# A rewritten head of a fused attention and two-layer kernel: parameters with the first keys, another order of loads and of TensorE's work, and the low parts of weights on GpSimd

## Chip, cores and metric

One core of one Trainium2 chip runs the whole program. The metric is device microseconds (us) of one execution; a profiled execution gives, beside its time, a span from its first to its last instruction and a trace of every engine. Engines are named as in the rows: PE is TensorE (PEld its weight loads), DVE is VectorE, ACT is ScalarE, POOL is GpSimd, SP is SyncE, which issues most transfers.

## The reference

Sliding-window attention with a few sink keys, then two dense blocks. Everything is in float32; the weights come in float64 and the two parameters as 64-bit integers (4 and 128 here).

```
B, H, S, D = 2, 8, 768, 64
scores = q @ k.T / sqrt(D)
keep = (key < n_sink) | ((query - key >= 0) & (query - key < window))
a = softmax(where(keep, scores, -1e9))           # with 1e-9 added to the sum
x = (a @ v), heads side by side                  # 1536 tokens x 512
h = x @ w_in                                     # 512 -> 2048
x = (relu(h) ** 2) @ w_out                       # 2048 -> 512
h = x @ w_in2
out = (P(h) / (Q(|h|) + 1e-6)) @ w_out2          # P cubic, Q quadratic
```

## The kernel before

**Tiling.** Tokens are cut into six segments of 256 (two blocks of 128 query rows), taken in three groups of 512 tokens. Attention works in units: one segment and one pair of heads (128 rows of x, chunk c of four). Group 0 has eight units; with two segments to a group, units 0 and 1 make chunk c = 0, units 2 and 3 chunk 1, and so on. Even units here begin a sequence (their first block sees 128 keys, the second 224), odd units see 224 keys in both blocks. Groups 1 and 2 are done later, in small steps among the dense matmuls of the group before.

**Precision.** A float32 product is made of three matmuls of high and low parts (gemm1_part, L476 to L478: whi by xhi, whi by xlo, wlo by xhi). So every x and every weight block is split. A weight block of 128x512 is converted from float64 in four steps (w_steps): top (ScalarE, L130), wt (VectorE, a shift and an or, L135), whi (ScalarE, L448), wlo = wt - whi (VectorE, L451). For x: high (ScalarE, L249) and low (VectorE, L253).

**The head** (L676 to L722) is the part that does the eight units of group 0, before the dense part starts. On ScalarE, VectorE and TensorE its instructions run in the order in which the program writes them (manual_schedule); GpSimd and SyncE are ordered by the framework's scheduler, and so is the dense part on ScalarE and VectorE. In step k of the loop, in this order: high of x of unit k-2; four masked maxima of unit k (VectorE, L203), which need the unit's scores; two exponentials (ScalarE, L209); one zero fill (L400) and the transposes of unit k-1 on TensorE (L226), copied out by ScalarE and VectorE (L231); two more exponentials; low of unit k-2; those parts of the first dense product (f = 0 and 1, chunk c) whose chunk satisfies c < (k-1) // 2 and whose weights are converted; the values of unit k-1 (L245); the scores of unit k+1 (L189); one step of a weight conversion (go); the sums of unit k and its scaling, first blocks on GpSimd and second blocks on VectorE (L220); two more steps of the conversion; from k = 1 to 7 the first step of the next conversion (begin). So seven conversions run in the head. When one ends, the next weight block is loaded.

**Before the loop.** SyncE issues keys and values of units 0 to 3 in turn, and then three weight blocks of 512 KB. The two parameters (nsw) come in a small transfer of their own on ScalarE's queue, spread to all partitions. setup builds the masks m0, m1, m2 from positions and parameters, mostly on VectorE (L300 to L331). TensorE runs 16 matmuls on zeros (fill, L400) and then the scores of unit 0.

**After the loop.** high and low of the last unit, and the parts that are left (both f, chunk 3), and then the dense part: for each f one first product (its first matmul at f = 2 here), ReLU and square (act1), and the second product two steps of f later. There the remaining weight blocks are converted, two for each f, while ScalarE and VectorE also serve the units of group 1. For such a conversion w_split may hold its instructions back behind an attention step recorded in va_hist.

## Time and profile before

| what | us |
|---|---|
| median of 3 runs (lowest, highest) | 628.69 (627.56, 628.84) |
| the profiled execution, its own time | 627.8 |
| its span, first to last instruction | 625.9 |
| busy: PE, DVE, ACT, POOL | 608.2, 412.8, 407.7, 112.9 |
| mean granted TensorE clock | 0.996 |

The span is what the rows below divide; 1.9 us of the execution's own time lie outside it. Ends of matmuls are modelled, so the busy time of PE is an upper figure. The shares of the whole span say little about the head, which is about a thirteenth of it.

### The profile page before, as it was taken

The page shows a single profiled execution, that of the slowest core. Times are in us where ns is not written, and L with a number is a line of the kernel's source. Part 1 is how long each engine was busy: PE and PEld are TensorE (multiplying, and loading weights), DVE is VectorE, ACT ScalarE, POOL GpSimd, SP SyncE. Part 2 cuts the span into 40 slices and gives each one's busy share as a digit, 9 for nine tenths or more (in the row PEclk, how much of TensorE's full clock was granted, in tenths as well). Part 3 has the DMA queues.
Part 4 walks back from the last instruction along what each step waited for, and adds up shares of the span by engine and source line. Part 5 has one row for each costly group of instructions (what it writes and reads, how often), then busy time and mean ns, then how long its engine had stood idle before and what let it go on. Part 6 is the DMA issues. An engine that isn't in the chain of part 4 may idle for free.

```text
span 625.9 us, 9412 instructions
## 1 busy us (share of the span) xinstructions
PE 608.2 (97%) x3465; PEld 485.6 (78%) x3465; DVE 412.8 (66%) x832; ACT 407.7 (65%) x838; POOL 112.9 (18%) x119
## 2 busy tenths in 40 slices
PE   7878999999999999999999999999999999999996
PEld 3556777777777777888888888888888888888884
DVE  5987787564333333247666469988998887877773
ACT  4778888575644444377777557777686666766662
POOL 2220101010000100030000013334234332222221
PEclk9999999999999999999999999999999999999999
DMA  8946576562222110023655300000010000100002
GB/s 292 302 147 205 181 271 208 190 198 59 79 59 71 52 30 30 2 67 135 203 201 183 121 1 0 2 0 1 2 67 1 1 1 0 69 0 1 0 2 71
DMA packets 19347, 54.80 MB, mean 88 GB/s; under 512 B 2528, under 2 KB 3808, under 8 KB 19296
## 3 DMA queue, kind: packets, MB, share of 16 engines
q1 hardware_dynamic: 19008, 54.01, 26.0%
q8 instruction: 29, 0.48, 0.3%
q14 instruction: 22, 0.18, 0.1%
q10 hardware_dynamic: 288, 0.13, 0.1%
HBM read 50.99 MB, written 3.15 MB: 86 GB/s over the span
## 4 chain that ended last, share of the span: by engine, by line
PE 89%; DVE 5%; ACT 3%; issue 1%; DMA 1%; DVEq 0%
PE b L476 14%; PE b L477 14%; PE b L478 13%; PE b L534 7%; PE b L536 7%; PE b L535 7%; PE b L497 7%; PE b L502 6%; PE b L498 6%; PE b L245 3%; PE b L189 2%; PE b L226 2%; DVE p L203 1%; ACT p L209 1%; DVE wt L135 1%
## 5 line engine op out<-in xcount | busy, mean ns | idle before, releaser
L476 PE MATMUL b<-xhi,whi 128*128 128x512 f32 x256 | 102.7, 402 | 1.4 <-ACT xhi L249 1.4
L477 PE MATMUL b<-xlo,whi 128*128 128x512 f32 x256 | 100.3, 392 | 3.6 <-DVE xlo L253 3.6
L478 PE MATMUL b<-xhi,wlo 128*128 128x512 f32 x256 | 99.9, 390 | 0.0
L525 POOL TENSOR_TENSOR glo<-t,ghi 128x512 fp32r<-128x512 f32 x34 | 48.4, 1424 | 228.9 <-ACT ghi L524 117.1
L488 DVE TENSOR_TENSOR glo<-b,ghi 128x512 fp32r<-128x512 f32 x48 | 33.2, 691 | 69.0 <-ACT b L487 68.8
L497 PE MATMUL b<-ghi,whi 128*128 128x512 f32 x192 | 76.7, 400 | 0.0
L498 PE MATMUL b<-ghi,wlo 128*128 128x512 f32 x192 | 74.9, 390 | 0.0
L535 PE MATMUL b<-wlo,ghi 128*128 128x512 f32 x192 | 74.7, 389 | 0.0
L534 PE MATMUL b<-whi,ghi 128*128 128x512 f32 x192 | 74.5, 389 | 0.0
L536 PE MATMUL b<-whi,glo 128*128 128x512 f32 x192 | 68.5, 389 | 0.0
L209 ACT ACTIVATE p<-p,mn 128x224 f32<-128x224 f32 (+1 forms) x96 | 44.0, 461 | 35.0 <-DVE mn L203 34.9
L220 POOL TENSOR_SCALAR p<-p,sums 128x224 f32<-128x224 f32 (+1 forms) x48 | 27.4, 582 | 217.6 <-DVE sums L215 158.9
L451 DVE TENSOR_TENSOR wlo<-wt,whi 128x512 fp32r<-128x512 f32 x64 | 44.0, 688 | 26.7 <-ACT whi L448 26.4
L477 PEld LDWEIGHTS b<-xlo,whi 128*128 128x128 f32 x256 | 48.1, 188 | 13.9 <-DVE xlo L253 4.9
L476 PEld LDWEIGHTS b<-xhi,whi 128*128 128x128 f32 x256 | 48.1, 188 | 12.6 <-ACT xhi L249 1.5
L448 ACT CAST whi<-wt 128x512 fp32r<-128x512 f32 x64 | 39.6, 619 | 26.2 <-PE b L477 15.3
L478 PEld LDWEIGHTS b<-xhi,wlo 128*128 128x128 f32 x256 | 48.0, 188 | 10.2
L130 ACT CAST top<-st 128x512 f16<-128x512 bf16 x64 | 49.6, 774 | 4.8 <-DVE wt L135 3.1
L502 PE MATMUL b<-glo,whi 128*128 128x512 f32 x192 | 52.2, 392 | 0.0
L478 PE MATMUL b<-yhi,wlo 128*128 128x512 f32 x128 | 49.8, 389 | 0.0
L476 PE MATMUL b<-yhi,whi 128*128 128x512 f32 x128 | 49.8, 389 | 0.0
L477 PE MATMUL b<-ylo,whi 128*128 128x512 f32 x128 | 49.8, 389 | 0.0
(128 smaller groups left out, 1181.7 us busy)
## 6 DMA issues: line engine op xcount, KB each, us to landing
st<-w SPq DMA_DIRECT2D x64, 512.0 KB, 3.4
vv<-att SPq DMA_DIRECT2D x12, 448.0 KB, 3.4
raw<-att SPq DMA_DIRECT2D x12, 352.0 KB, 3.1
out<-o SPq DMA_DIRECT2D x8, 256.0 KB, 2.0
raw<-att SPq DMA_DIRECT2D x6, 272.0 KB, 3.9
vv<-att SPq DMA_DIRECT2D x6, 256.0 KB, 4.1
raw_e<-att SPq DMA_DIRECT2D x4, 352.0 KB, 5.3
vb<-att SPq DMA_DIRECT2D x4, 256.0 KB, 4.7
```

The source lines that it names most:

```text
L130: nc.scalar.copy(top.bitcast(F16).rearrange("p (n w) -> p n w", w=2)[:, :, 1], head)
L209: self.f.lastA = self.nc.scalar.activation(p, p, AF.Exp, scale=-1.0, bias=self.mn[i, k], accum_out=self.sums[:, j : j + 1])
L476: nc.tensor.matmul(h[:, :n], whi[:, cs], xhi[:, c, :n], start=(c == 0), stop=False)
L477: nc.tensor.matmul(h[:, :n], whi[:, cs], xlo[:, c, :n], start=False, stop=False)
L478: nc.tensor.matmul(h[:, :n], wlo[:, cs], xhi[:, c, :n], start=False, stop=(c == NC - 1))
L497: nc.tensor.matmul(acc[m], whi[:, ms], ghi, start=(f == 0), stop=False)
L498: nc.tensor.matmul(acc[m], wlo[:, ms], ghi, start=False, stop=False)
L502: nc.tensor.matmul(acc[m], whi[:, ms], glo, start=False, stop=(f == NF - 1))
L525: self.lastL = nc.gpsimd.tensor_tensor(glo, t3, ghi.bitcast(F32), op=ALU.subtract)
L534: nc.tensor.matmul(acc[t], ghi[:, ts_], whi, start=(f == 0), stop=False)
L535: nc.tensor.matmul(acc[t], ghi[:, ts_], wlo, start=False, stop=False)
L536: self.lastM = nc.tensor.matmul(acc[t], glo[:, ts_], whi, start=False, stop=(f == NF - 1))
```

## The change

- The parameters are appended to the first unit's keys (four words on each partition) and arrive with them; their own transfer is gone.
- The loads before the loop go in the order of FIRST: k is the next unit's keys and queries, v the next unit's values, w a weight block. The three weight loads in step 0 are gone from there.
- The masks: positions outside the causal range are set to a large distance ahead of the parameters (far), so that one comparison with the window does both tests. first_mask (two parameter steps, a copy, m0) stands after the scores of unit 0; second_mask after the second maximum of unit 0, with m1 on VectorE and m2 on GpSimd.
- The zero fills: 6 instead of 16 ahead of the first scores, 8 instead of 1 ahead of the transposes of unit 0, and 3 new ones ahead of its values.
- The parts of the first product follow c < (k-2) // 2, a unit later; in the last step high, low and the rest of the parts stand directly behind the values of the last unit. That pair of instructions is recorded in va_hist.
- Conversions begin in steps 0 to 6 instead of 1 to 7, and in the head their last step (wlo) is done by GpSimd. In the dense part it stays on VectorE.
- Small tiles: nsw and neg are gone, pad (32 bytes on each partition) and up are new, nabs is made earlier.

Left out of the diff: the other path of the program for other parameters, which reads the same packed array, and bookkeeping of widths and arguments.

```diff
@@ -44,6 +44,7 @@
 PER = 3
 HEAD = 2
 DEPTH = 4
+FIRST = "kkvkwvkwvwv"
 NALT = 4
 LAG = 2
 LAG2 = 3
...
@@ -109,7 +116,10 @@
             s = r.start
             vv += [np.concatenate([pad, x[:NSK], x[s : s + D]], axis=0) for x in heads]
             vv += [np.concatenate([x[s - D : s], x[:NSK], pad], axis=0) for x in heads]
-        parts += [np.concatenate(kq, axis=0).reshape(-1), np.concatenate(vv, axis=1).reshape(-1)]
+        kq = np.concatenate(kq, axis=0)
+        if not parts:
+            kq = np.concatenate([kq, np.tile(nsw.view(kq.dtype), (P, 1))], axis=1)
+        parts += [kq.reshape(-1), np.concatenate(vv, axis=1).reshape(-1)]
     return np.ascontiguousarray(np.concatenate(parts))
 
...
@@ -280,12 +290,11 @@
         for top in self.tops:
             nc.gpsimd.memset(top, 0)
         self.ident = c.tile([P, P], F32, name="ident")
-        self.nsw = c.tile([P, 4], I32, name="nsw")
         self.nswf = c.tile([P, 4], F32, name="nswf")
+        c.tile([P, 8], F32, name="pad")
         self.par = c.tile([P, 2], F32, name="par")
         self.ab = c.tile([P, 6], F32, name="ab")
-        io = self.io
-        nc.scalar.dma_start(self.nsw, io["nsw"].bitcast(I32).partition_broadcast(P))
+        self.nabs = c.tile([P, 2], F32, name="nabs")
         make_identity(nc, self.ident)
...
                        allow_small_or_imprecise_dtypes=True)
         v = nc.vector
-        f = self.nswf
-        t = c.tile([P, 2], F32, name="neg")
-        v.tensor_copy(f, self.nsw)
-        lo = f.rearrange("p (s w) -> p s w", w=2)[:, :, 0:1]
-        hi = f.rearrange("p (s w) -> p s w", w=2)[:, :, 1:2]
-        t3 = t.rearrange("p (s w) -> p s w", w=1)
-        p3 = self.par.rearrange("p (s w) -> p s w", w=1)
-        v.tensor_scalar(t3, lo, 0.0, 4294967296.0, op0=ALU.is_lt, op1=ALU.mult)
-        v.tensor_tensor(t3, t3, lo, op=ALU.add)
-        v.scalar_tensor_tensor(p3, in0=hi, scalar=4294967296.0, in1=t3, op0=ALU.mult, op1=ALU.add)
-        ns, win = self.par[:, 0:1], self.par[:, 1:2]
+        lo_, hi_ = slice(0, D), slice(D, P)
+        sk, skh = slice(P, KB), slice(D, D + NSK)
+        for rows, cs, x in ((lo_, slice(KB, WQ), NSK), (hi_, slice(0, D), -D), (hi_, slice(D + NSK, WQ), NSK - D)):
+            v.tensor_scalar_add(rel[rows, cs], rel[rows, cs], float(x))
+        for t in (rel0, rel):
+            far = tmp("wlo4_1", t.shape[-1])
+            v.tensor_scalar(far, t, 0.0, BIG, op0=ALU.is_lt, op1=ALU.mult)
+            v.tensor_tensor(t, t, far, op=ALU.max)
+        v.memset(rel[lo_, sk], BIG)
         self.m0 = c.tile([P, P], F32, name="m0")
         self.m1 = c.tile([P, WQ], F32, name="m1")
         self.m2 = c.tile([P, WQ], F32, name="m2")
-        self.nabs = c.tile([P, 2], F32, name="nabs")
-        m0, m1, m2 = self.m0, self.m1, self.m2
-        out, fut0, fut = tmp("wlo4_1", P), tmp("whi5_0", P), tmp("wlo5_0", WQ)
-        lo_, hi_ = slice(0, D), slice(D, P)
-        for rows, cs, x in ((lo_, slice(KB, WQ), NSK), (hi_, slice(0, D), -D), (hi_, slice(D + NSK, WQ), NSK - D)):
-            v.tensor_scalar_add(rel[rows, cs], rel[rows, cs], float(x))
-        v.tensor_scalar(fut0, rel0, 0.0, -BIG, op0=ALU.is_lt, op1=ALU.mult)
-        v.tensor_scalar(fut, rel, 0.0, -BIG, op0=ALU.is_lt, op1=ALU.mult)
-        v.tensor_scalar(m0, rel0, win, -BIG, op0=ALU.is_ge, op1=ALU.mult)
-        v.tensor_tensor(m0, m0, fut0, op=ALU.min)
-        v.tensor_scalar(out, col, ns, -BIG, op0=ALU.is_ge, op1=ALU.mult)
-        v.tensor_tensor(m0, m0, out, op=ALU.max)
-        v.tensor_scalar(m2, rel, win, -BIG, op0=ALU.is_ge, op1=ALU.mult)
-        v.tensor_tensor(m2, m2, fut, op=ALU.min)
-        sk = slice(P, KB)
-        v.tensor_copy(m2[hi_, D : D + NSK], out[hi_, :NSK])
-        v.tensor_copy(m1, m2)
-        v.tensor_tensor(m1[lo_, :NSK], m1[lo_, :NSK], out[lo_, :NSK], op=ALU.max)
-        v.memset(m1[lo_, sk], -BIG)
-        v.tensor_copy(m2[lo_, sk], out[lo_, :NSK])
+        raw = self.raw0
+        f, par = self.nswf, self.par
+        lo, hi = (f.rearrange("p (s w) -> p s w", w=2)[:, :, i : i + 1] for i in range(2))
+        t3 = c.tile([P, 2], F32, name="up").rearrange("p (s w) -> p s w", w=1)
+        p3 = par.rearrange("p (s w) -> p s w", w=1)
+        ns, win = par[:, 0:1], par[:, 1:2]
+
+        def first_mask():
+            v.tensor_copy(f, raw[:, raw.shape[-1] - 4 :].bitcast(I32))
+            v.scalar_tensor_tensor(t3, in0=lo, scalar=0.0, in1=hi, op0=ALU.is_lt, op1=ALU.add)
+            v.scalar_tensor_tensor(p3, in0=t3, scalar=4294967296.0, in1=lo, op0=ALU.mult, op1=ALU.add)
+            v.tensor_scalar(rel0, rel0, win, -BIG, op0=ALU.is_ge, op1=ALU.mult)
+            v.scalar_tensor_tensor(self.m0, in0=col, scalar=ns, in1=rel0, op0=ALU.is_ge, op1=ALU.mult)
+
+        def second_mask():
+            m1, m2, G = self.m1, self.m2, nc.gpsimd
+            v.tensor_scalar(m1, rel, win, -BIG, op0=ALU.is_ge, op1=ALU.mult)
+            v.scalar_tensor_tensor(m1[lo_, :NSK], in0=col[lo_, :NSK], scalar=ns[lo_], in1=m1[lo_, :NSK],
+                                   op0=ALU.is_ge, op1=ALU.mult)
+            v.tensor_scalar(m1[hi_, skh], col[hi_, :NSK], ns[hi_], -BIG, op0=ALU.is_ge, op1=ALU.mult)
+            G.tensor_scalar(m2, rel, win, -BIG, op0=ALU.is_ge, op1=ALU.mult)
+            for rows, cs in ((lo_, sk), (hi_, skh)):
+                G.tensor_scalar(m2[rows, cs], col[rows, :NSK], ns[rows], -BIG, op0=ALU.is_ge, op1=ALU.mult)
+
+        self.masks = [first_mask, second_mask]
         nu = 2 * sum(u[2][2] for u in units())
         self.mn = c.tile([P, nu], F32, name="mn")
         self.mn_i = 0
...
         return [f"{p}{c + i}_{k}" for i in range(2) for k in range(2) for p in ("whi", "wlo")]
 
     def att_load(self, u, early, alt):
-        wk, wq = seg_dims(u[2])[:2]
-        w = wk + wq
+        w = raw_width(u)
         if early is not None:
             raw = self.yp.tile([P, self.yw[early]], F32, tag=f"y{early}", name="raw_e")[:, :w]
         else:
             raw = self.att.tile([P, w], F32, tag="raw", name="raw", bufs=2)
         off = self.att_off[u]
+        if not off:
+            self.raw0 = raw
         self.lastD = self.nc.sync.dma_start(raw, self.io["att"][off : off + P * w].rearrange("(p w) -> p w", w=w))
         return raw
 
     def att_load_v(self, u, alt):
         tags = self.alt_tags(alt)
         wk, wq, wa, wb = seg_dims(u[2])
-        off = self.att_off[u] + P * (wk + wq)
+        off = self.att_off[u] + P * raw_width(u)
         src = self.io["att"][off : off + P * (wa + wb)].rearrange("(p w) -> p w", w=wa + wb)
         if alt:
             out = [self.att_tile("va", wa, alt=tags[3]), self.att_tile("vb", wb, alt=tags[4])]
...
@@ -448,7 +461,7 @@
             nc.scalar.copy(out[0], t)
 
         def low():
-            nc.vector.tensor_tensor(out[1], t, out[0].bitcast(F32), op=ALU.subtract)
+            last.tensor_tensor(out[1], t, out[0].bitcast(F32), op=ALU.subtract)
             self.w[(which, f, half)] = tuple(out)
 
         return [lambda: f64_top(nc, st, top), lambda: f64_rest(nc, st, t, top), high, low]
...
         nload = 0
 
-        def prefetch():
+        def prefetch(values=True):
             nonlocal nload
             if nload < len(us):
                 g0 = us[nload][0] == 0
                 early = (None, 0, 1, 2)[nload % DEPTH] if g0 else None
                 u, alt = us[nload], nload % NALT if g0 else 0
-                raws = [self.att_load(u, early, alt), None]
-                if g0:
-                    raws[1] = self.att_load_v(u, alt)
-                loaded.append((u, raws))
+                loaded.append((u, [self.att_load(u, early, alt), None]))
                 nload += 1
+                if g0 and values:
+                    values_of(nload - 1)
+
+        def values_of(i):
+            u, raws = loaded[i - nload]
+            raws[1] = self.att_load_v(u, i % NALT)
 
         n0 = sum(1 for u in us if u[0] == 0)
         done = 0
@@ -645,8 +660,13 @@
             self.w_split(which, f, half)
             wload(which)
 
-        for _ in range(DEPTH):
-            prefetch()
+        for i, what in enumerate(FIRST):
+            if what == "k":
+                prefetch(values=False)
+            elif what == "v":
+                values_of(FIRST[:i].count("v"))
+            else:
+                wload(0)
         self.setup()
 
         self.new_x(0)
@@ -661,9 +681,14 @@
             un[k] = Unit(self, *loaded.pop(0), k % NALT)
             un[k].scores([self.bank(b) for b in SCB[k % 2]])
 
+        def pieces(n):
+            for f, c in [x for x in parts if x[1] < n and (0, x[0], 0) in self.w]:
+                self.gemm1_part(0, f, c, self.x[0], GN[0], hb[f])
+                parts.remove((f, c))
+
         def begin():
             key = cq[0].pop(0)
-            conv.append(self.w_steps(*key))
+            conv.append(self.w_steps(*key, nc.gpsimd))
             conv[0].pop(0)()
 
         def go():
@@ -676,22 +701,23 @@
         pinned = ExitStack()
         pinned.enter_context(tc.manual_schedule(engines={E.PE}))
         with tc.manual_schedule(engines={E.Activation, E.DVE}):
-            self.fill(self.bank(0), 16)
+            self.fill(self.bank(0), 6)
             scores(0)
+            self.masks[0]()
             for k in range(n0 + 1):
                 cur, prev, old = un.get(k), un.get(k - 1), un.get(k - 2)
-                if k == 0:
-                    wload(0, 3)
                 if old:
                     old.high()
                 ex = list(cur.blocks) if cur else []
                 for i, j in ex:
                     cur.maximum(i, j)
+                    if not k and (i, j) == (0, 1):
+                        self.masks[1]()
                 for i, j in ex[:2]:
                     cur.exponential(i, j)
                 if prev:
                     tb = [self.bank(b) for b in (0, 1)]
-                    self.fill(tb[0], 1)
+                    self.fill(tb[0], 8 if k == 1 else 1)
                     for j in range(2):
                         prev.transpose(j, tb[j])
                         prev.copy(j)
@@ -699,13 +725,18 @@
                     cur.exponential(i, j)
                 if old:
                     old.low()
-                for f, c in [x for x in parts if x[1] < (k - 1) // pairs and (0, x[0], 0) in self.w]:
-                    self.gemm1_part(0, f, c, self.x[0], GN[0], hb[f])
-                    parts.remove((f, c))
+                pieces((k - 2) // pairs)
                 if prev:
-                    prev.values(self.bank(SCB[k % 2][0]))
+                    ob = self.bank(SCB[k % 2][0])
+                    if k == 1:
+                        self.fill(ob, 3)
+                    prev.values(ob)
                 if k + 1 < n0:
                     scores(k + 1)
+                if k == n0:
+                    high = prev.high()
+                    self.va_hist.append((prev.low(), high))
+                    pieces(NC)
                 go()
                 if cur:
                     cur.sum()
@@ -713,15 +744,12 @@
                         cur.scale(i, j)
                 go()
                 go()
-                if 0 < k <= NCONV:
+                if k < NCONV:
                     begin()
                 while nload < n0 and len(loaded) < DEPTH - 1 or not loaded:
                     prefetch()
-            un[n0 - 1].high()
-            un[n0 - 1].low()
+            assert not parts
             done = n0
-        for f, c in parts:
-            self.gemm1_part(0, f, c, self.x[0], GN[0], hb[f])
```

## Rows read from the trace of the kernel before

**Rows 1.** Busy time by stretch: engines, granted clock, share of DMA, GB/s.

```profile
8.40:50.60 42.20, 32.26 (x376) 22.33 (x369) 35.33 (x131) 32.13 (x98) 10.05 (x16) 0.96 0.73 249
50.60:90.00 39.40, 38.84 (x246) 30.18 (x246) 29.59 (x72) 34.42 (x78) 3.49 (x6) 1.00 0.68 222
200.00:626.00 426.00, 419.69 (x2025) 344.79 (x2017) 290.55 (x450) 272.39 (x496) 87.24 (x68) 1.00 0.14 47
```

**Rows 2.** Timeline of DVE: start, duration, what, idle before and its releaser.

```profile
5.19 0.17 DVE L300 CAST nswf<-nsw 128x4 f32<-128x4 int32 x1 [2.44 <-DMA nsw<-nsw]
...
6.04 0.29 DVE L320 TENSOR_SCALAR m<-tmp,par 128x128 f32<-128x128 f32 x1
...
8.40 0.28 DVE L203 CUSTOM_DVE_ANT_0 p<-b,m 128x128 f32<-128x128 f32 x1
...
16.32 0.29 DVE L203 CUSTOM_DVE_ANT_0 p<-b,m 128x128 f32<-128x128 f32 x1 [0.71 <-PE b L189]
...
25.02 0.67 DVE L451 TENSOR_TENSOR wlo<-wt,whi 128x512 fp32r<-128x512 f32 x1
...
29.44 0.67 DVE L451 TENSOR_TENSOR wlo<-wt,whi 128x512 fp32r<-128x512 f32 x1
```

**Rows 3.** Loads issued at 0.75 and 3.07: size, us to landing.

```profile
raw<-att SPq DMA_DIRECT2D x1, 272.0 KB, 4.3
...
raw_e<-att SPq DMA_DIRECT2D x1, 272.0 KB, 5.9
```

**Rows 4.** Timeline of PE.

```profile
1.00 6.55 PE L400 MATMUL b<-zero 128*128 128x512 bf16 x16 [1.00 <-POOL zero L277]
...
25.75 1.04 PE L226 MATMUL b<-ident,p 128*128 128x128 f32 x8
...
28.62 0.99 PE L189 MATMUL b<-raw_e 64*64 64x224 f32 x16
...
49.95 0.40 PE L476 MATMUL b<-xhi,whi 128*128 128x512 f32 x1
...
50.65 0.39 PE L476 MATMUL b<-xhi,whi 128*128 128x512 f32 x1
```

**Rows 5.** The chain that ended last: start, duration, what.

```profile
14.79 1.38 PE b L189 x16
...
21.10 0.38 DVE p L203
...
25.73 0.29 DVE p L203
...
30.04 0.38 DVE p L203
...
34.47 0.83 PE b L189 x16
35.37 0.29 DVE p L203
...
39.67 0.38 DVE p L203
```

**Rows 6.** Waits of PE, 0 to 130 us: total, times, longest.

```profile
PE b L477 <- DVE xlo L253: 3.6, 4, 1.1
...
PE b L226 <- DVE mn L203: 0.6, 1, 0.6
```

**Rows 7.** Timeline of POOL in the head.

```profile
11.14 0.78 POOL L220 TENSOR_SCALAR p<-p,sums 128x128 f32<-128x128 f32 x2 [8.57 <-DVE sums L215]
...
20.03 1.30 POOL L220 TENSOR_SCALAR p<-p,sums 128x128 f32<-128x128 f32 x2 [4.10 <-DVE sums L215]
```

**Rows 8.** Busy time in one stretch, columns as in rows 1.

```profile
14.00:17.00 3.00, 3.00 (x34) 2.04 (x31) 1.81 (x9) 1.60 (x6) 0.97 (x2) 0.50 1.04 390
```

**Rows 9.** One line of the kernel on POOL: ns min/median/max, first and last start.

```profile
L525 POOL TENSOR_TENSOR glo<-t,ghi x34: 1287/1302/2165, 356.2 to 611.3; 128x512 fp32r<-128x512 f32 x34
```

**Rows 10.** Timeline of ACT at the head's end.

```profile
47.49 0.76 ACT L130 CAST top<-st 128x512 f16<-128x512 bf16 x1
```

More of the change, by code (lines that the diff above doesn't have):

```diff
@@ L86, in units, with raw_width, pack_attention @@
     return out
-def pack_attention(q, k, v):
+def raw_width(u):
+    wk, wq = seg_dims(u[2])[:2]
+    return wk + wq + (4 if u == units()[0] else 0)
+def pack_attention(q, k, v, nsw):
     qT = q.transpose(0, 1, 3, 2)
@@ L433, in w_split_, with w_steps @@
     def w_split_(self, which, f, half):
-        for step in self.w_steps(which, f, half):
+        for step in self.w_steps(which, f, half, self.nc.vector):
             step()
-    def w_steps(self, which, f, half):
+    def w_steps(self, which, f, half, last):
         nc = self.nc
@@ L567, in run @@
             self.att_off[u] = off
-            wk, wq, wa, wb = seg_dims(u[2])
-            off += P * (wk + wq + wa + wb)
+            off += P * (raw_width(u) + sum(seg_dims(u[2])[2:]))
         self.yw = [NC * GN[0], NC * GN[1], 2 * TG2]
```

18 lines of the change are left out of this document (9 added, 9 removed).

## Prediction

> **What bounds the kernel now.** I read the table of busy time by stretch first [rows 1]. In the last 426 us TensorE is busy for 419.69, so nothing that the change touches in the head can make that part shorter; it can only start earlier. From 50.6 to 90 us TensorE is nearly full too (38.84 of 39.40), with ScalarE at 34.42. In the head, 8.4 to 50.6, TensorE is busy for 32.26 of 42.20 us, VectorE for 35.33: this is where time can be had, and there the order on ScalarE and VectorE is written out by hand, one unit after the other. So I followed one unit's beat, from the first maximum of one unit (L203) to that of the next, and asked of each beat which wait ends last.
>
> The start: VectorE can do nothing with the parameters before 5.19, when their small load has landed, and then runs nineteen small instructions for masks and parameters, so that the first maximum comes at 8.40 [rows 2], although the first scores need only the first key load, landed at 0.75 + 4.3 = 5.05 [rows 3]. TensorE passes that time in 16 zero fills that take 0.41 us each [rows 4]. Matmuls of the same 512 columns advance by 0.23 us later on (three from 49.95 to 50.65) [rows 4], so the fills run at the lower level, 1.2 GHz.
>
> The beats start at 21.10, 25.73, 30.04, 35.37 and 39.67 [rows 5]: 4.63, 4.31, 5.33 and 4.30 us for units 3 to 6. In the odd ones TensorE waits for the low part of x that VectorE has only just made: four such waits, 3.6 us in all [rows 6]. In the even ones VectorE is the limit: it ends its scaling and then subtracts a weight's low part, 0.60 us from its start to that of the next maximum (29.44 to 30.04) [rows 2, 5].
>
> **The change, part by part.** All times are of the profiled execution.
>
> *Start.* The parameters ride with the first keys, so they land at about 5.05 instead of 5.19. Behind them stand three small operations and two of 128 columns instead of nineteen: 5.19 to 6.04 is four such small steps (0.2 each), the wide ones 0.3 each [rows 2], so the first mask is ready at 5.05 + 0.6 + 0.6 = 6.25. The work on positions moves ahead of the landing, into VectorE's idle 2.4 us. Scores of unit 0 start at 5.05; with 6 fills (ended near 3.5) TensorE is then idle for 1.5 us, and I take the lower level, 1.38 us against 0.83 for such 16 matmuls [rows 5]: 6.45, and the first maximum at 6.6, 1.8 us earlier. The second mask puts three operations (about 0.7) between the second and third maximum; the exponentials trail the maxima, so I count 0.4: **-1.4**. Its other half goes to GpSimd, idle there until its scaling. Bounds: three such operations take 1.2 us at 0.39 each (half of the pair of 0.78) [rows 7] and, at 1.3 each, 3.9; even then it is ready at 10.2, when unit 1's maxima need it.
>
> *Loads.* In the new order the first weight block is fifth in the queue, behind 1152 KB. The sixth load now ends the first 1600 KB and lands at 3.07 + 5.9 = 9.0 [rows 3]; the new fifth ends 1664 KB, so 9.2. Now ScalarE takes that block at the end of unit 0, ahead of unit 1's exponentials, at about 9.1 to 9.9. Unit 1's first maximum is due at 10.2. The load is hidden unless it comes later than about 9.9; from there each us costs one, as all exponentials queue behind it.
>
> *Units 1 and 2.* Between 14 and 17 us the granted clock was 0.50 [rows 8], after TensorE had waited for unit 0's scaling, whose GpSimd part starts at 11.14 [rows 7]. The scores in it took 1.38, the same 0.83 later [rows 5]. Eleven new fills (8 ahead of the transposes, 3 ahead of the values) stand in exactly that wait; at 0.41 each the 8 end by 11.5, when the transposes' input is ready from 10.5 and their first copy is due 11.7. I take the full clock from there on: 0.55 from the scores and, by the same ratio, 0.5 from the values, less 0.3 for fills that run over: **-0.7**. The third unit's first maximum then comes at 14.2 instead of 16.32 [rows 2]. Unit 2, 16.32 to 21.10, loses VectorE's 0.60 and the rest of the low clock and is held by TensorE alone, from the transposes to the end of the scores 28.62 + 0.99 - 25.75 = 3.86 [rows 4], about 4.1 with the waits: **-0.7**.
>
> *The low part on GpSimd and the parts of the first product.* VectorE's beat without the subtraction is 25.02 - 21.10 = 3.92 for odd units, 29.44 - 25.73 = 3.71 for even ones [rows 2, 5]. The parts now come one unit later, in even units: the odd ones lose the wait for x, units 3 and 5 go to 3.95: 0.68 + 1.38 = **-2.1**. The even ones now carry six of these matmuls where unit 4 had three. From its transposes at 25.75 to the end of its scores it needed 3.86 us; three more at 0.23 are 0.69, of which 0.1 falls in a wait: 4.45 against 4.31 and 4.30, so **+0.3**. GpSimd takes 1.30 us for such a subtraction (median; longest 2.17) [rows 9]. With its scaling that is 2.1 to 2.8 of 4 us, behind the scaling, and over before the next scaling; nothing waits for the low part in that time.
>
> GpSimd's pair of scalings took 0.78 at 11.14, and 1.30 at 20.03, where VectorE's subtraction with both inputs in SBUF came behind its own scaling [rows 7]. So 0.5 us of the wait ahead of the transposes goes too; that is what keeps the even beat at 4.45. The Trainium skill, SBUF — State Buffer, section "Who interferes with whom", says that a VectorE instruction with two SBUF inputs and a GpSimd instruction that reads SBUF shut each other out for a whole instruction, whoever comes first. By that rule, the trace agrees; it also speaks against this change, since a longer GpSimd instruction now holds what VectorE's scaling and its shift-and-or need. By the rows the sum stays as it is, by the rule at its worst it is the first rival below.
>
> *The end of the head.* Unit 7 loses its parts (beat 3.95). Then transposes 1.04, six matmuls 1.4 in what was a wait for the copies, values 1.15. Before, two ScalarE steps of weights stood ahead of the last xhi (the second 0.76 at 47.49) [rows 10], and TensorE waited; in the new order xhi and xlo follow the values at once, and 2.2 us later the parts are done. From unit 7's first maximum: 3.9 + 3.6 + 2.1 = 9.6 against 50.65 - 39.67 = 11.0 [rows 4, 5]: **-1.4**.
>
> Head: -1.4 - 0.7 - 0.7 - 2.1 + 0.3 - 1.4 = **-6.0**.
>
> *What is late next.* The new last unit does no weight conversion, and none may start ahead of x's last low part. Before, an eighth was under way at 47.49 [rows 10]. The dense part starts one to one and a half conversions poorer. One costs ScalarE 0.76 [rows 10] and about 0.6, so 0 to 2.1 us. TensorE was already a little late there (a wait of 0.6 for a unit's maxima) [rows 6], and ScalarE has 5 us of air in 39.4 [rows 1]. I take **+1.3**. The dropped and added small tiles shift addresses; same-shaped operations show no spread that I could tie to an address, so nothing.
>
> **Sum**: -6.0 + 1.3 = -4.7. The profiled execution took 627.8 (span 625.9 and 1.9 around it) and would take 623.1; the median of the runs is 0.9 above it, 628.69, so **624.0**. A measurement here tells about 0.2% (1.3 us) from no change.
>
> **Rivals.**
> 1. *GpSimd's subtraction shuts VectorE out (slower).* If it is put ahead of the scaling (GpSimd's order isn't written by hand) or runs into the next shift-and-or, VectorE waits up to 1.30 in each of seven units: at 1.0, 7.0 us, so 631. It decides from 4.7 / 7 = 0.67 per unit. Against it: the scaling's input is ready before the weight's high part, and about 1.2 us of air lie between its end and the next shift-and-or.
> 2. *TensorE stays at the lower level.* Ten early fills are gone, and TensorE is idle from 3.5 to 5.05. A unit has some 3 us of TensorE work; at 1.38 / 0.83 that is 2 us more, partly hidden. Up to the end of unit 3: +3.3, so 627.3. For it: one idle stretch was enough for 14 to 17 [rows 8]. Against it: from 5.05 TensorE now has work without a break.
> 3. *The dense part gives it back.* Conversions bind it, and TensorE waits there as long as the head was shortened, but for a us: 628. The wait of 0.6 speaks for it, ScalarE's air against.
> 4. *Nothing is late:* the lag costs nothing and the clock rises at once: 622.
>
> **Chances.** Forecast 0.62 (its own range 622.4 to 626.5: the lag 0 to 2.1, the clock up to unit 2, fills that run over); rival 1 0.08; rival 2 0.12; rival 3 0.12; rival 4 0.06. The range that leaves out rival 1 and the outer parts of 3 and 4: 621.6 to 628.4. Faster by over 0.2% (below 627.4): forecast, rival 4 and four fifths of rival 2, 0.78. Within: 0.14. Slower: 0.08.
>
> **What would show it.** First maximum at 6.6 (not before 8); granted clock of 1 by the first values; beats of 4 us in odd and 4.5 in even units, no TensorE wait for xlo but the last; GpSimd's subtractions at 1.3 right behind its scalings; first matmul of the third gemm block near 44.7 instead of 50.65, and TensorE waits of 1 to 2 us between there and 85. Wrong if VectorE's scaling or shift-and-or stretches above 1 us, if the clock is at 0.5 beyond 12 us, or if those later waits grow to 4.

## The result, and the profile after

| | before | after |
|---|---|---|
| median of 4 runs, us (lowest, highest) | 628.12 (627.36, 628.84) | 622.00 (621.27, 622.59) |
| profiled execution, its span | 627.8, 625.9 | 621.27, 619.4 |
| end of the head's parts, us from the span's start | 50.65 | 44.55 |
| what is left of the span behind that | 575.26 | 574.82 |
| of this: to the start of the last matmul, and behind it | 568.65, 6.6 | 569.01, 5.8 |

The ratio is 0.9906 (95%: 0.9888 to 0.9924): faster by 6.1 us of the median, where 4.7 were forecast. The time is in the predicted range (621.6 to 628.4), 2.0 us below the predicted 624.0 and just below the forecast's own range of 622.4 to 626.5. The median before is 628.12 here and was 628.69 when the prediction was made.

In the changed kernel the first maximum is L213, a fill L413, the transposes L236, scores L199, values L255, the parts of the first product L489 to L491, the conversion's four steps L140, L145, L461 and L464, and high and low of x L259 and L263.

Busy time by stretch, the head, what follows it, and the first part of what follows (`44.30:60.00`; columns as in [rows 1]):

```profile
5.33:44.55 39.22, 31.98 (x386) 21.93 (x379) 31.15 (x123) 30.67 (x96) 16.81 (x26) 1.00 0.76 280
44.55:84.00 39.45, 39.31 (x248) 30.55 (x247) 31.38 (x74) 35.63 (x80) 3.71 (x6) 1.00 0.67 225
44.30:60.00 15.70, 15.70 (x82) 12.47 (x81) 12.23 (x28) 15.46 (x33) 1.17 (x2) 1.00 0.60 204
```

The like stretch of the kernel before, as long and as far from the end of its head:

```profile
50.40:66.10 15.70, 15.70 (x82) 12.45 (x80) 11.04 (x25) 12.78 (x29) 1.32 (x2) 1.00 0.58 189
```

Against [rows 1] the head (from the first maximum on) is 3 us shorter, GpSimd does 6.8 us more in it and VectorE 4.2 less. Behind it TensorE is as full as it was (39.31 of 39.45). From the end of the head to the last matmul the kernel now takes 0.36 us more, with one new wait for ScalarE (four of 16 scores start at 84.75, the other twelve at 85.39). At the very end it takes 0.8 us less, because the last store lands sooner (before, then after):

```profile
85.39 0.81 PE L199 MATMUL b<-raw 64*64 64x128 f32 x12 [0.20 <-ACT x L408]
```

```profile
out<-ot SPq DMA_DIRECT2D x1, 128.0 KB, 3.7
```

```profile
out<-ot SPq DMA_DIRECT2D x1, 128.0 KB, 2.8
```

The change doesn't touch that store, and it took between 2.8 and 3.7 us in the fourteen traces of this document. So the span, 6.5 us shorter, gained 6.1 in the head, lost 0.4 behind it and owes 0.8 to the last store.

The start, on VectorE and TensorE, and two loads in the chain of waits, the first keys and the fourth weight block (the last two lines: start, duration, what):

```profile
3.52 0.17 DVE L327 CAST nswf<-raw 128x4 f32<-128x4 int32 x1 [0.48 <-DMA raw<-att]
...
5.33 0.29 DVE L213 CUSTOM_DVE_ANT_0 p<-b,m 128x128 f32<-128x128 f32 x1 [0.15 <-PE b L199]
```

```profile
1.00 2.74 PE L413 MATMUL b<-zero 128*128 128x512 bf16 x6 [1.00 <-POOL zero L287]
3.67 1.45 PE L199 MATMUL b<-raw 64*64 64x128 f32 x16
...
6.02 1.90 PE L413 MATMUL b<-zero 128*128 128x512 bf16 x8
9.23 0.91 PE L236 MATMUL b<-ident,p 128*128 128x128 f32 x6 [1.31 <-POOL p L230]
```

```profile
0.75 2.75 DMA raw<-att
...
13.92 7.79 DMA st<-w
```

The first keys are there at 3.50, not at 5.05 as in [rows 3]. From there to the first maximum it takes 1.83 us (3.39 before), and scores, not masks, end last, by little: the mask is ready at 5.17. The pace of the scores is still that of the lower level, 1.45 for 16 against 0.83 (the column of the granted clock reads 1.00 from the start, so here the pace has to tell).

GpSimd and VectorE around the first maxima of unit 3, and the waits of TensorE from 0 to 130 us:

```profile
16.40 0.78 POOL L230 TENSOR_SCALAR p<-p,sums 128x128 f32<-128x128 f32 x2 [1.63 <-DVE sums L225]
17.15 1.27 POOL L464 TENSOR_TENSOR wlo<-wt,whi 128x512 fp32r<-128x512 f32 x1
```

```profile
19.27 0.68 DVE L145 SCALAR_TENSOR_TENSOR wt<-st,top 128x512 int32<-128x512 int32 x1
```

```profile
PE b L255 <- ACT pT L241: 4.2, 5, 1.1
PE b L236 <- POOL p L230: 2.1, 2, 1.3
...
PE b L489 <- ACT xhi L259: 0.5, 1, 0.5
PE b L199 <- ACT x L408: 0.2, 1, 0.2
```

The subtraction follows the scaling at once, takes 1.27 and ends at 18.42, 0.85 us before VectorE's shift-and-or, which keeps its 0.68. The pair of scalings takes 0.78, as at 11.14 in [rows 7]. The four waits for xlo of [rows 6] are gone; the one for xhi is the only such wait left.

The head by the prediction's steps (first maximum of each unit; a unit's beat runs from its first maximum to that of the next):

| step | before | after | predicted change | measured |
|---|---|---|---|---|
| first maximum of unit 0 | 8.40 | 5.33 | -1.8 | -3.07 |
| first maximum of unit 2 | 16.32 | 13.14 | -2.1 | -3.18 |
| beat of unit 2 | 4.78 | 4.07 | -0.7 | -0.7 |
| beat of unit 3 | 4.63 | 3.93 | -0.7 | -0.7 |
| beat of unit 4 | 4.31 | 5.15 | +0.1 | +0.8 |
| beat of unit 5 | 5.33 | 3.93 | -1.4 | -1.4 |
| beat of unit 6 | 4.30 | 4.62 | +0.2 | +0.3 |
| unit 7's first maximum to the end of the parts | 10.98 | 9.69 | -1.4 | -1.3 |
| end of the head to the last matmul | 568.65 | 569.01 | +1.3 | +0.4 |
| last matmul to the end of the span | 6.6 | 5.8 | 0 | -0.8 |

Four rows are off: the start, unit 4 and the last two. One experiment or more stands against each of the first three. In the start, unit 0's beat grew by 0.68 (3.21 to 3.89), where the prediction counted 0.4 for the second mask. Unit 4's is in the timeline of ScalarE:

```profile
21.79 0.79 ACT L140 CAST top<-st 128x512 f16<-128x512 bf16 x1 [1.19 <-DMA st<-w]
...
22.70 0.40 ACT L219 ACTIVATE p<-p,mn 128x128 f32<-128x128 f32 x1
```

The first maximum was there at 21.15, but its exponential is queued behind the first step of the fourth weight block, issued at 13.92 and landed 7.79 us later, at 21.71.

### The profile page after: what moved, and what is told of

It reads as the page before. It is cut to its first block, busy times and chain, and to the rows that moved or that the text cites. A ratio compares the mean times of both kernels' runs of the same rounds, so it can differ in the third digit from the quotient of the medians.

```text
span 619.4 us, 9428 instructions
## 1 busy us (share of the span) xinstructions
PE 605.4 (98%) x3465; PEld 484.4 (78%) x3465; DVE 408.3 (66%) x821; ACT 406.8 (66%) x838; POOL 120.7 (19%) x129
## 4 chain that ended last, share of the span: by engine, by line
PE 87%; ACT 6%; DVE 3%; DMA 2%; issue 1%; POOL 0%; DVEq 0%; ACTq 0%
PE b L489 14%; PE b L490 13%; PE b L491 13%; PE b L548 7%; PE b L547 7%; PE b L549 7%; PE b L510 7%; PE b L515 6%; PE b L511 6%; PE b L255 3%; PE b L236 2%; PE b L199 2%; ACT p L219 2%; ACT top L140 1%; DMA st<-w 1%
## 5 line engine op out<-in xcount | busy, mean ns | idle before, releaser
L489 PE MATMUL b<-xhi,whi 128*128 128x512 f32 x256 | 102.7, 402 | 0.5 <-ACT xhi L259 0.5
L491 PE MATMUL b<-xhi,wlo 128*128 128x512 f32 x256 | 99.9, 390 | 0.0
L230 POOL TENSOR_SCALAR p<-p,sums 128x224 f32<-128x224 f32 (+1 forms) x48 | 24.4, 519 | 202.1 <-DVE sums L225 130.4
L489 PEld LDWEIGHTS b<-xhi,whi 128*128 128x128 f32 x256 | 48.1, 188 | 11.8 <-issue 1.3
L464 DVE TENSOR_TENSOR wlo<-wt,whi 128x512 fp32r<-128x512 f32 x57 | 39.3, 689 | 25.9 <-ACT whi L461 25.5
L491 PEld LDWEIGHTS b<-xhi,wlo 128*128 128x128 f32 x256 | 48.1, 188 | 10.4
L461 ACT CAST whi<-wt 128x512 fp32r<-128x512 f32 x64 | 39.6, 619 | 22.5 <-PE b L490 15.3
L140 ACT CAST top<-st 128x512 f16<-128x512 bf16 x64 | 49.6, 775 | 5.8 <-DVE wt L145 4.6
L491 PE MATMUL b<-yhi,wlo 128*128 128x512 f32 x128 | 49.8, 389 | 0.0
L489 PE MATMUL b<-yhi,whi 128*128 128x512 f32 x128 | 49.8, 389 | 0.0
```

The lines of the kernel that those rows point to most:

```text
L140: nc.scalar.copy(top.bitcast(F16).rearrange("p (n w) -> p n w", w=2)[:, :, 1], head)
L489: nc.tensor.matmul(h[:, :n], whi[:, cs], xhi[:, c, :n], start=(c == 0), stop=False)
L491: nc.tensor.matmul(h[:, :n], wlo[:, cs], xhi[:, c, :n], start=False, stop=(c == NC - 1))
```

## The experiments

Theory: the head sets all. The parameters with the keys, the low part on GpSimd, the parts a unit later and the fills each shorten it, and ScalarE's air makes up the late conversions. Rivals: the gain is one part's alone; GpSimd's work shuts VectorE out; the clock falls; the dense part gives back; addresses count. Spans and head ends are of one profiled execution of each kernel; ratios are to the kernel before, run on the same chip. A ratio is uncertain by about 0.18%, so two kernels that lie within some 1.6 us of each other are told apart by their traces alone. Three parts of the change were not undone alone: the order of the loads, the shorter masks and the new order in the last step of the head. What they brought is read from the changed kernel's trace and not shown by a run.

**The low part back on VectorE.**

```diff
-            conv.append(self.w_steps(*key, nc.gpsimd))
+            conv.append(self.w_steps(*key, nc.vector))
```

> Only the subtraction of the weights' low parts goes back to VectorE in the head; all else stays as changed. If VectorE's length is what the change relieved: the beats of units 2 to 6 grow by 0.4 to 0.6 us each, GpSimd's pair of scalings takes 1.3 again instead of 0.8, and the whole is 2 to 3 us slower than the changed kernel (span 621.5 to 622.5). Rival, ScalarE's order sets the beat and VectorE was only next to it: beats within 0.1, whole within 0.5 us (span 619 to 620).

624.23 us, ratio 0.9937 (0.9921 to 0.9953). The beats of units 1 to 6 are 4.51, 4.28, 4.52, 4.56, 4.53, 4.55. In four of them the next maximum follows VectorE's subtraction at once; those of units 4 and 6 end with scores or GpSimd's scaling, 0.1 to 0.2 us behind it. Odd units lose 0.6 us; of the even ones only unit 2 loses (0.2), so the expected 0.4 to 0.6 for each did not come. GpSimd's scalings are slow again, as the pair of 1.30 in [rows 7], and TensorE waits six times for them where it waited twice:

```profile
26.39 0.67 DVE L464 TENSOR_TENSOR wlo<-wt,whi 128x512 fp32r<-128x512 f32 x1
```

```profile
25.92 1.30 POOL L230 TENSOR_SCALAR p<-p,sums 128x128 f32<-128x128 f32 x2 [3.03 <-ACT whi L461]
30.53 1.46 POOL L230 TENSOR_SCALAR p<-p,sums 128x224 f32<-128x224 f32 x2 [3.31 <-ACT whi L461]
```

The head ends at 47.77, 3.2 later: 1.36 up to unit 7's first maximum and 1.86 behind it. Some of the latter is not the edit: there the granted clock was 0.73 (39 to 42.5 us) and 0.70 (to 45), and six parts took 2.5 us instead of 1.6. The ratios give 1.9 us for the edit, as much as for the sixteen fills below and more than for the other three parts of the head that were undone alone (0.6 to 1.3).

**The parts of the first product a unit earlier, as before.**

```diff
-                pieces((k - 2) // pairs)
+                pieces((k - 1) // pairs)
```

> Only the rule for the parts of the first product goes back to c < (k-1) // 2. If the wait for the low part of x was worth what the prediction says: TensorE waits about 1 us for xlo again in units 3, 5 and 7, the even units lose 0.3 to 0.5, whole +1.5 to +2.5 us (span 621 to 622). Rival, the matmuls are only moved from one beat to the next: within 0.5 us of 619.4.

622.89 us, 0.9918 (0.9901 to 0.9935); head 46.55, 2.0 later. Beats of units 3 and 5 are 5.35 and 5.36, 1.4 longer each, those of units 4 and 6 are 0.3 and 0.6 shorter, and the waits for x are back:

```profile
PE b L490 <- DVE xlo L263: 3.4, 3, 1.1
```

So the step "parts a unit later" holds in kind, and in the traces in size; the ratios differ by 0.8 us only, which they can't tell from 2.

**Fewer fills: one ahead of the first transposes, none ahead of the values.**

```diff
-                    self.fill(tb[0], 8 if k == 1 else 1)
+                    self.fill(tb[0], 1)
-                        self.fill(ob, 3)
+                        self.fill(ob, 0)
```

> Only the fills of the second step go back (1 and 0 instead of 8 and 3); the first 6 stay. If they hold the clock: granted clock 0.5 for 3 to 4 us somewhere between 9 and 16 us, scores of unit 2 at 1.4 instead of 0.83, first maximum of unit 2 about 1 us later, whole +1 us (span 620.4). Rival, the clock holds without them: no stretch at 0.5, and the whole is 0 to 0.5 us faster, as transposes and values need not queue behind them.

622.79 us, 0.9916 (0.9899 to 0.9933). The profiled execution is the longest of its six; its head ends at 47.66, with beats of 4.95 and 6.70 in units 1 and 2:

```profile
11.00:13.00 2.00, 1.93 (x24) 1.65 (x28) 1.52 (x5) 2.00 (x7) 0.46 (x1) 0.50 1.05 401
13.00:15.00 2.00, 2.00 (x21) 1.16 (x14) 1.05 (x8) 0.89 (x5) 1.74 (x3) 0.50 1.07 388
15.00:18.00 3.00, 2.62 (x23) 2.10 (x23) 1.98 (x6) 1.94 (x8) 0.00 (x0) 0.50 0.75 273
```

The clock is at 1.2 GHz from about 10.5 us, after TensorE had been 2.05 us without work, to beyond 20. The ratios make it 0.6 us, and the other five executions are 0.5 to 2.1 us shorter than the profiled one, so not every execution need pay the whole price.

**The small spread load back.** Four words to each partition, on ScalarE's queue as in the kernel before, into a new tile that nothing reads.

```diff
+        spare = c.tile([P, 4], I32, name="spare")
+        nc.scalar.dma_start(spare, self.io["a"].bitcast(I32).partition_broadcast(P))
         make_identity(nc, self.ident)
```

> A transfer of 16 bytes, spread to all partitions, is issued on ScalarE's queue at the start as before the change, into a tile that nobody reads; the parameters still come with the keys. If that small transfer was what held the first keys up: they land at about 5 us again instead of 3.5, first maximum at 6.7 instead of 5.33, whole +1 to +1.5 us (span 620.5 to 621). Rival, the new order on SyncE's queue (keys ahead of values) makes the first keys earlier: landing stays at 3.5 and the whole within 0.5 us of 619.4.

625.24 us, 0.9952 (0.9934 to 0.9971): a larger loss than the head shows. The first keys land at 4.90, the head ends 0.9 later (45.45), and what is left behind it is 578.63, 3.8 longer than in the changed kernel (3.0 up to the last matmul, 0.8 behind it, where the last store took 3.4 us). The new tile also moves every tile allocated behind it. So the two were parted.

**The same load, into the 32 bytes of pad, so that no tile moves.**

```diff
-        c.tile([P, 8], F32, name="pad")
+        spare = c.tile([P, 8], I32, name="spare")
+        nc.scalar.dma_start(spare[:, :4], self.io["a"].bitcast(I32).partition_broadcast(P))
```

> The small spread load of the run before it again, but into the 32 bytes of the pad tile, so that no other tile moves. In that run the head ended 0.9 us later and the dense part took 3.8 us more. If the dense part's 3.8 us came from the moved tiles and not from the load: first keys land near 4.9, first maximum near 6.7, head ends at 45.4, the rest takes 574.9 as in the changed kernel, span 620.3. Rival, the load itself disturbs the later part: the rest 578 or more again, span 624.

622.79 us, 0.9926 (0.9908 to 0.9943). The first keys (of these two loads the first; size, us to landing after an issue at about 0.75) need 4.0 us instead of 2.75:

```profile
raw<-att SPq DMA_DIRECT2D x1, 274.0 KB, 4.0
spare<-a ACTq DMA_DIRECT2D x1, 2.0 KB, 4.2
```

The first maximum comes at 6.61 (1.83 behind the landing, as in the changed kernel), the head ends at 45.50, and what is left is 574.95. So the small load alone held the keys up, for about 1 us of time; the 3.0 us up to the last matmul in the run before came from the moved tiles (1.6 by the ratios), as that stretch is 568.94 here.

**No pad, and a pad that is 512 bytes larger.**

```diff
-        c.tile([P, 8], F32, name="pad")
```
```diff
-        c.tile([P, 8], F32, name="pad")
+        c.tile([P, 8 + 128], F32, name="pad")
```

> Only the pad tile of 32 bytes is taken out; the tiles behind it move down. If TensorE's pace depends on where its operands lie: matmuls of the second block's first product step at 233 ns instead of 227 (384 of them, 2.6 us), and the rest behind the head takes 577 to 579 instead of 574.9 (span 621.5 to 623.5); the head itself unchanged at 44.5. Rival, addresses do nothing and the earlier run's slow part had another cause: 574.9 and a span of 619.4.

> The pad tile is 512 bytes longer, so that everything behind it moves by 512 bytes. If only the place within 512 bytes counts for TensorE's pace: steps at 227 ns, span 619.4 as in the changed kernel. Rival, any move of the tiles away from where they were costs: steps at 233 ns somewhere and a span of 621 or more.

No pad: 625.32 us, 0.9955 (0.9937 to 0.9973), with 578.56 behind the head, 3.7 more, all but 0.1 of it up to the last matmul. Larger pad: 622.07 us, 0.9911 (0.9894 to 0.9927), with 574.87. Groups of TensorE's instructions from 44 us on (busy time and mean ns of one), in the changed kernel, without the pad, and with the larger one:

```profile
L491 PE MATMUL b<-yhi,wlo 128*128 128x512 f32 x128 | 49.8, 389 | 0.0
L489 PE MATMUL b<-yhi,whi 128*128 128x512 f32 x128 | 49.8, 389 | 0.0
```

```profile
L488 PE MATMUL b<-yhi,whi 128*128 128x512 f32 x128 | 50.7, 396 | 0.0
L490 PE MATMUL b<-yhi,wlo 128*128 128x512 f32 x128 | 50.6, 396 | 0.0
```

```profile
L491 PE MATMUL b<-yhi,wlo 128*128 128x512 f32 x128 | 49.8, 389 | 0.0
L489 PE MATMUL b<-yhi,whi 128*128 128x512 f32 x128 | 49.8, 389 | 0.0
```

From start to start these matmuls advance by 226.5 to 227 ns in the changed kernel and with the larger pad, by 233 to 234 without the pad and with the spare tile. There are 384 of them: about 2.5 of the 3.7 us; the rest is spread thinly over others. Moves by 16 and by 32 bytes cost it, a move by 512 bytes doesn't, so what counts repeats after 512 bytes (or 64, 128 or 256, which no run tells apart). Which tile it is wasn't isolated. The kernel before has 389 ns here too: the pad gains nothing, it keeps what the dropped tiles would have lost. (Without the pad the head ended 1.9 later, but 1.6 of that lies behind unit 7's first maximum, where the granted clock was 0.53 from 39 to 42.5 us.)

**The coefficients with the first keys.** Two more small spread loads (a and b of the second block, 2 and 1 KB) are issued at 12.28 and 13.35, ahead of the fourth weight block. Here they ride with the first keys too, six more words on each partition.

```diff
-    return wk + wq + (4 if u == units()[0] else 0)
+    return wk + wq + (10 if u == units()[0] else 0)
...
+            G.tensor_copy(self.ab, raw[:, raw.shape[-1] - 6 :])
             G.tensor_scalar(m2, rel, win, -BIG, op0=ALU.is_ge, op1=ALU.mult)
...
-        nc.sync.dma_start(ab[:, 0:4], io["a"].partition_broadcast(P))
-        nc.sync.dma_start(ab[:, 4:6], io["bb"].partition_broadcast(P))
```

> The six coefficients of the second block also come with the first keys, and GpSimd copies them out; their two small spread loads, issued at 12.3 and 13.4 us in the changed kernel, are gone. If those two hold the queue ahead of the fourth weight block (landed 21.7, for which ScalarE waited 1.2 us and unit 4's beat was 5.15): it lands near 19.7, ScalarE doesn't wait, beat of unit 4 at 4.6, whole -0.5 us (span 618.9). Rival, the queue is full with large loads and the block lands at 21 or later anyway: beat stays at 5.1, span 619.4.

620.96 us, 0.9891 (0.9873 to 0.9909). The weight block is issued at 12.99 and lands at 20.34, 1.4 us earlier, 0.9 of it because it is issued earlier; ScalarE takes it without a wait, unit 4's beat is 4.62 and the head ends at 44.20. The span, 620.0 where 618.9 was expected, doesn't show it: the last store took 3.7 us here and 2.8 in the changed kernel; up to the last matmul (568.92) nothing was lost. The ratios don't tell the two apart. Busy time from 17 to 18 us, the changed kernel first (the last two columns are the share of the DMA engines and GB/s):

```profile
17.00:18.00 1.00, 1.00 (x11) 0.73 (x7) 0.78 (x5) 0.82 (x3) 1.00 (x2) 1.00 0.26 78
```

```profile
17.00:18.00 1.00, 1.00 (x15) 0.74 (x7) 0.72 (x4) 0.81 (x3) 1.00 (x2) 1.00 1.10 416
```

So 3 KB in small pieces left the engines mostly idle for a us in the middle of 512 KB loads. The run with the larger pad, with the program order of the changed kernel, shows the same stall at another length (1.86 and a beat of 5.81).

**The low part subtracted twice on GpSimd**, so that it occupies 2.6 us a unit. It computes the same values.

```diff
+            for _ in range(1 if last is nc.vector else 2):
-            last.tensor_tensor(out[1], t, out[0].bitcast(F32), op=ALU.subtract)
+                last.tensor_tensor(out[1], t, out[0].bitcast(F32), op=ALU.subtract)
```

> GpSimd makes each low part in the head twice, so 2.6 us instead of 1.3 for each unit. If it has air there and does not shut VectorE out: beats within 0.1 of 3.93 and 4.62, head ends within 0.4 of 44.5 us, span 619 to 620. Rival, the two engines hold each other up: the second subtraction lies over VectorE's shift-and-or or over the next scaling, one of these stretches by 0.5 us or more, beats grow by 0.3 to 1.0, head ends at 46.5 to 51.

624.20 us, 0.9950 (0.9934 to 0.9965). GpSimd's two subtractions and VectorE's shift-and-or, in two units:

```profile
18.39 2.62 POOL L465 TENSOR_TENSOR wlo<-wt,whi 128x512 fp32r<-128x512 f32 x2
...
22.95 2.65 POOL L465 TENSOR_TENSOR wlo<-wt,whi 128x512 fp32r<-128x512 f32 x2
```

```profile
20.47 1.09 DVE L145 SCALAR_TENSOR_TENSOR wt<-st,top 128x512 int32<-128x512 int32 x1
...
24.67 1.48 DVE L145 SCALAR_TENSOR_TENSOR wt<-st,top 128x512 int32<-128x512 int32 x1
```

GpSimd is done at 21.01 and 25.60, the shift-and-or 0.55 later in both, nearly its whole 0.68: it did not run slowly, it waited. The Trainium skill, SBUF — State Buffer, section "Who interferes with whom", says that the pair of ports which the two engines share is an exclusive lock, held for the whole instruction by whoever issues first. By that rule the shift-and-or waits until GpSimd is done; the trace agrees, with 0.55 us of it behind that. So rival 1's mechanism exists. It starts when GpSimd's work lasts until the next shift-and-or; the 1.27 of the changed kernel ends 0.85 us ahead of it. The head ends 1.8 later (46.35), of which 1.25 is unit 1's beat of 5.17, at a low clock (below); the beats of units 3 and 5 grew by 0.25 and 0.43, and unit 4's lost its wait for the load (4.62). The ratios make it 2.8: the profiled execution is the shortest of its six, and what the others lost no trace shows.

**An eighth conversion in the head.**

```diff
-NCONV = 7
+NCONV = 8
```

> The last unit's step begins an eighth conversion, so that the dense part starts with one more. If the lag of the conversions costs time in the dense part (the prediction took 1.3 us): the rest behind the head takes 573.5 to 574.3 instead of 574.8, the head at most 0.3 more. Rival, ScalarE makes the lag up by itself: the rest 574.8 as before, whole within 0.4 us of 619.4.

622.11 us, 0.9921 (0.9898 to 0.9943); 574.47 behind the head against 574.82, and 568.79 against 569.01 up to the last matmul. A conversion in stock is worth 0.2 us there, and nothing in the median: a lag of 1.3 isn't there. (The wait for ScalarE at 85 us stays. The head ends 0.6 later, not 0.3 at most, with unit 1's beat at 5.17 at a low clock, below.)

**Sixteen fills ahead of the first scores, as before.**

```diff
-        self.fill(self.bank(0), 6)
+        self.fill(self.bank(0), 16)
```

> Only the first fills go back to 16. If they stand ahead of the first scores as TensorE's order has it: scores of unit 0 at 7.5 instead of 3.67, at the higher level, first maximum at 8.3 to 8.5 instead of 5.33, and with it the head and the whole about 3 us later (span 622.5). Rival, units 1 and 2 win back what the first loses, as the clock is up earlier and the fills of the second step are then too many: +1 us or less.

623.48 us, 0.9938 (0.9915 to 0.9961). The fills end at 6.36, the scores run at the full clock (0.83 instead of 1.45), and the first maximum comes at 7.15 instead of 5.33. That is earlier than the expected 8.3 to 8.5, because the 16 fills took 5.36 us and not the 6.55 of [rows 4]. The head ends 1.3 later: of the 1.8 lost at the start unit 4 gives 0.5 back, as its weight block has landed by then (beat 4.63). The higher level doesn't pay for the wait. (The span is longer by 2.4, as the last store took 3.7 us here too.)

**The best version: coefficients with the keys, and the parts shared out**, those of f = 0 in even and of f = 1 in odd units, where TensorE waits 1.05 us for the copy.

```diff
-        def pieces(n):
-            for f, c in [x for x in parts if x[1] < n and
+        def pieces(n, fs=(0, 1)):
+            for f, c in [x for x in parts if x[0] in fs and x[1] < n and
...
-                pieces((k - 2) // pairs)
+                pieces((k - 2) // pairs, (0, 1) if k == n0 else (k % 2,))
```

> The version with the coefficients in the first keys, and the parts of the first product shared out: f = 0 in even units, f = 1 in the odd unit behind, where TensorE waits 1.05 us for a copy. If the even beats of 4.62 are TensorE's, lengthened by six matmuls, and three of them fit into that wait: beats of units 4 and 6 near 3.95, odd ones unchanged at 3.93, head ends 1.2 to 1.4 us earlier (42.8 to 43.0), whole -1.2 us against that version (span 618 to 618.8). Rival, the three only lengthen the odd beats by as much as they leave the even ones: within 0.3 us of it.

620.64 us, 0.9890 (0.9870 to 0.9910). Even beats are 4.08 (4.62), odd ones stay at 3.94, as expected: 1.1 us. The profiled execution lost 1.2 of it again in unit 1 (5.13, granted clock 0.51 from 11 to 13 us), so its head ends at 44.29. It is the fastest measured, but its interval holds the changed kernel's ratio too.

**The clock in unit 1.** In four traces the beat of unit 1 was 4.95 to 5.17 and the clock 0.50 or 0.51 from 11 to 13 us; in the other nine it was 3.9 to 4.5, at 1.00. The waits of the first transposes part them (the run with two subtractions, then the best version; the changed kernel's, 1.31, is shown with its start):

```profile
3.67 0.88 PE L199 MATMUL b<-raw 64*64 64x128 f32 x16
...
9.24 0.91 PE L236 MATMUL b<-ident,p 128*128 128x128 f32 x6 [2.02 <-POOL p L230]
```

```profile
3.67 1.06 PE L199 MATMUL b<-raw 64*64 64x128 f32 x16
...
9.35 0.91 PE L236 MATMUL b<-ident,p 128*128 128x128 f32 x6 [2.00 <-POOL p L230]
```

In the four (few fills 2.05, eight conversions 1.85, and these two) TensorE was idle for 1.85 to 2.05 us ahead of the transposes, in the other nine for 0.3 to 1.61. In three of the four that came from a good start: the clock rose early, the first scores took 0.83 to 1.06 instead of 1.45, and the eight fills, a fixed number, were through sooner. No run changed the idle time alone, and at the head's end the clock fell in two traces after waits (1.05 and 0.84) that the changed kernel has at the same place without it. So what decides is left open.

## Why the prediction was right, and where its sizes were off

- **Start (-1.4).** The chain behind the landing shrank by 1.56 us (3.39 to 1.83): by its own figures, the prediction had 3.35 to 1.55. Mis-sized is the landing, taken as unchanged at 5.05; it is 3.50, because the small spread load is gone, and with that load back it is 4.78. (The work on positions was to be over before the landing; with keys that early some of it stands behind, eleven small operations instead of five, but the scores end later still.) Mis-sized too is the second mask, 0.68 in unit 0's beat and not 0.4. By the beginning of unit 2 the gain is 3.18 instead of 2.1.
- **Loads ("hidden").** Right for the first weight block. Wrong for the fourth, which the prediction didn't look at: it stands behind the two loads of coefficients, and a ScalarE step that waits for it holds the exponentials. It is the mechanism the prediction described for the first block, three blocks later; it cost 0.5 to 0.7 us.
- **Units 1 and 2.** Unit 1's beat fell by 0.8 (4.71 to 3.92), predicted 0.7; unit 2's is 4.07, predicted 4.1. The clock is at 1.00 in the changed kernel's trace, and without the new fills it is at 0.50 from about 10.5 to beyond 20 us.
- **Low part on GpSimd, parts a unit later (-2.1 + 0.3).** Undone alone, the parts cost 2.0 us of the head in the trace; the low part costs 1.4 up to unit 7's first maximum (1.9 of the whole by the ratios). As the prediction has it, the odd units need both: 3.93 becomes 5.35 without the one and 4.5 without the other. Odd beats 3.93 (3.95 predicted); even ones 4.62 (4.45), which are TensorE's, as moving three matmuls to where it waits brings them to 4.08.
- **End of the head (-1.4).** 9.69, predicted 9.6.
- **What is late next (+1.3).** Mis-sized: it measured +0.4. ScalarE made up most of the conversions in the first 16 us behind the head, busy for 15.46 of 15.70 where the kernel before has 12.78, and TensorE lost nothing there. Of the TensorE waits of 1 to 2 us expected between 45 and 85 only the one at its end is there, at 85, and it costs 0.6 from start to start; the 0.6 that the kernel before waited for maxima [rows 6] is gone. An eighth conversion brings 0.2.
- **Last store (no term).** 0.8 of the profiled gain is luck: the last store landed sooner. Start, unit 4, the lag and the store (about -1.1, +0.7, -0.9 and -0.8) make up the 1.8 us by which the profiled execution came out below the 623.1 foreseen.
- **Addresses ("nothing").** Right for this change only because the pad is in it; without the pad it would have been +3.7 by the traces and +3.1 by the ratios. The prediction did not see what the pad is for, so this was right by luck.
- **Rivals.** GpSimd shutting VectorE out needs twice the subtraction. The lower clock does occur, in three versions that keep all fills, at about 1.2 us. The dense part gave 0.4 back. "Nothing is late" (622, chance 0.06) named the time, and it is nearer than the forecast in the lag, which costs 0.4; but the clock had not risen at once (the first scores took 1.45), and the time met it only because the misses at the start, at unit 4 and at the last store add up to about -1.2. That is luck.

## What to carry to other kernels

Where the first block of a kernel sets all that follows, follow its beats and ask of each which wait ends last: in the traces each edit here was worth what its own beat showed, and the bulk behind started sooner, within 0.4 us. Before a difference of a us in one trace is put down to an edit, look at the end of the span too: the last store alone moved it by 0.9. Look at every small spread load ahead of a large one, not only at those on the path. When a small tile is dropped or added, look at the pace of the matmuls far behind it: a few words moved can cost more than the edit gains.

## What the runs showed of the hardware

- A load of 16 bytes to each of 128 partitions held the landing of the 274 KB issued beside it up from 2.75 to 4.0 us; behind two such loads (16 and 8 bytes) the DMA share fell to 0.26 for a us, against 1.10 without them.
- A VectorE instruction with two inputs in SBUF waits for GpSimd's subtraction: the shift-and-or of 0.68 us lasted 1.09 and 1.48 and ended 0.55 behind it. The other way round, GpSimd's pair of scalings takes 1.30 instead of 0.78 beside VectorE's subtraction.
- The 384 matmuls of 512 columns in the second block's first product advance by 227 ns, and by 233 after small tiles moved everything behind them by 16 or 32 bytes; a move by 512 bytes leaves 227.
- A store of 128 KB at the end of the program landed after 2.8 to 3.7 us, with nothing changed about it.
- In the four traces where TensorE had idled for 1.85 to 2.05 us ahead of the first transposes the clock fell to 0.50, in the nine with 0.3 to 1.61 it did not; in three of the four the idle time was longer because a fixed number of fills stood behind scores that ran faster (0.83 to 1.06 us instead of 1.45). The idle time was not varied alone.
